# Other places in the instruction streams for four small pieces of a fused retention and MLP kernel: the first constants, a first ScalarE copy, the splits of the feature halves, the loads of the second weight

## The chip, the cores and the metric

The kernel runs on one core of one Trainium2 chip. The metric is the device time of one execution in microseconds (us); several runs are taken and their median is given. Besides them one execution is recorded by the hardware profiler, and every row below is from that execution. An engine is named as the profile names it: PE is TensorE's matmuls, PEld its weight loads, DVE is VectorE, ACT is ScalarE, POOL is GpSimd, and SP is SyncE, the engine that issues all DMAs of this kernel (SPq is its queue).

## The reference, cut to what matters

```python
# retention: 4 batches, 8 heads, 576 positions, 64 dims per head
ret = (q @ k.T / sqrt(64)) * gamma[h] ** (i - j)   # zero above the diagonal
x = ret @ v                                        # (4, 576, 512)
# first MLP with a spatial gate
h = gelu_tanh(x @ w_in); u, v = halves(h)
v = (v - mean) / sqrt(var + 1e-6) * g_ln
x = x + (u * (w_sg @ v + b_sg)) @ w_out
# second MLP
xn = (x - mean) / sqrt(var + 1e-6) * g_ln
out = x + relu(xn @ w_ch1) @ w_ch2                 # 512 -> 2048 -> 512
```

Everything is fp32. The kernel computes each product of the two MLPs as three matmuls of split operands, hi*hi + hi*lo + lo*hi, where hi is a rounded copy of an operand and lo the remainder. Such a split costs an ACT copy (hi) and a DVE or POOL subtraction (lo).

## The kernel before, in words

**Retention (about the first 90 us).** Sixteen units (4 batches by 4 pairs of heads) are worked on one after the other. A unit needs its tile of q, k and v, called ld (`load_unit`, L183), and the constants of its pair of heads, called tab (`load_tab`, L432): decay masks and scales. `prep_unit` (L195) scales k on ACT with a column of tab (L207), `scores` (L209) multiplies k and q on PE (L219) and masks the result on DVE with tab (L224), `states` (L234) builds the running state from the scaled k (PE L240, ACT L246, DVE L248), and `attend` (L263) puts the pieces together. Unit 0 is loaded in three pieces: half of the positions of q and k (256 KB), the other positions (320 KB), the rest of the tile (544 KB). Every other unit is one DMA of 1120 KB, and every tab one of 225.5 KB. At the start the order on SP is: unit 0, tab 0, unit 1, tab 1, unit 2, tab 2, tab 3 (L435 to L438). Then DVE zeroes a tile and PE multiplies it three times (L440 to L444) before the first unit is prepared.

**First MLP (to about 311 us).** It is not touched by the change.

**Second MLP (from about 311 us).** The 18 row tiles are cut into 3 blocks (`NB`), and each block takes 8 steps (`NQ`). A step s makes two chunks of 128 hidden features for 768 rows: `hidden` (L946) computes them by a 7-product scheme (Strassen's, on 2 by 2 blocks) in four parts, and `project` (L975) multiplies the hidden chunks of step s - 1 by their part of w_ch2. The loop over s has an inner loop over four quarters q (L1050 to L1075). In a quarter the program emits one part of `hidden`, one `project`, and then the preparation of weights: in quarter 0 `split_w2` and `load_w2` of one half of w_ch2 and the first part of `split_w1` (ACT L727, DVE L728), in quarter 1 the second part of `split_w1` (ACT L727, POOL L728) and `load_w1`, in quarter 2 `split_w2` and `load_w2` of the other half, in quarter 3 the four POOL sums of `mix_w1` (L714 to L718) for the weights of step s + 2. `split_w2` is an ACT copy (L741) and a POOL subtraction (L742); `load_w2` (L730) is one DMA of 256 KB into one of two buffers, the one that the split before it has read. w_ch2 is loaded three quarters or more before it is split.

Last in a quarter comes `ahead(blk, q)` (L1009), where q now counts the 32 quarters of a block. It prepares the next block: rows are loaded and normed, their transposes written to DRAM (L765) and read back (L777), scaled (L785), and in the last quarters of a block turned into the 7 operands of the scheme. Four of the operands are differences (`mix_features`, L796, POOL L799, called m0 to m3 here), and each of the 7 is split (`split_features`, L802, ACT L806 and DVE L807): first the plain quarter b11, then m0, m1, m2, m3, then the plain b21 and b22. In block 0 `ahead` also does the last of the conversions of w_ch from 64-bit to 32-bit (DVE L142 to L151, written to DRAM by L371), whose buffers are given to the operands of block 1 at its quarter 24 (L1028 to L1034).

All engines run their instructions in the order in which the program emits them, so the place of a call in this loop is its place in the queue of its engine. In part (1, 2) of `hidden`, DVE adds product 2 from a PSUM bank (L964), and the next part goes on accumulating into that same bank, so PE has to wait for that L964.

Of the kernel before, what the change touches and what calls it, by code (L numbers as in the profile page):

```python
# [21 lines left out]
NP = H // 2  # L22
# [69 lines left out]
def kernel(  # L92
# [12 lines left out]
    nc = tc.nc  # L105
    ctx.enter_context(tc.manual_schedule())
    act, dve, pool, pe = nc.scalar, nc.vector, nc.gpsimd, nc.tensor
# [51 lines left out]
    def bank():  # L159

        return banks.popleft()
# [13 lines left out]

    tab = [pa.tile([128, TA], F32, tag=f"tab{hp}", bufs=1, name=f"tab{hp}") for hp in range(NP)]

    NU = B * NP
    units = {}
    xb = {}  # L180
# [2 lines left out]
    def load_unit(n):  # L183
        t = ld.tile([128, AW], F32, tag="ld", name="ld")
        if n == 0:

            to, src = (z[:, 0:2 * S].rearrange("p (a s) -> p a s", a=2) for z in (t, attn[n]))
            for x, y in ((0, 2 * C), (2 * C, S)):
                nc.sync.dma_start(out=to[:, :, x:y], in_=src[:, :, x:y])
            nc.sync.dma_start(out=t[:, 2 * S:], in_=attn[n, :, 2 * S:])  # L190
        else:
            nc.sync.dma_start(out=t, in_=attn[n])
        units[n] = dict(ld=t)
# [235 lines left out]
            mm3(ps, hi[:, k, c], lo[:, k, c], wi[k][:, 0, 512:], wi[k][:, 1, 512:], k == 0, k == KE - 1)  # L429
        return ps  # L430

    def load_tab(hp):  # L432
        nc.sync.dma_start(out=tab[hp], in_=tab_in[hp])

    for n in range(3):  # L435
        load_unit(n)
        load_tab(n)
    load_tab(NP - 1)  # L438

    zero = pa.tile([128, 512], F32, tag="p", name="zero")  # L440
    dve.memset(zero, 0.0)
    warm = bank()
    for _ in range(WARM):
        pe.matmul(warm, zero[:, 0:128], zero, start=True, stop=True)  # L444
# [4 lines left out]
    states(0)  # L449
    for n in range(NU):  # L450
        if n + 3 < NU:
            load_unit(n + 3)
# [277 lines left out]
    def load_w2(s):  # L730
        if s < NB * NF:
            if t2 is None:
                w2_raw[s] = x_raw[2][:, WQ - 1024 + s * 512:WQ - 1024 + (s + 1) * 512]
            else:
                w2_raw[s] = t2.tile([128, 512], F32, tag="w2", bufs=2, name="raw_w2")
            nc.sync.dma_start(out=w2_raw[s], in_=w2_dram[s % NF // 2 + NQ * (s % 2)])

    def split_w2(s):
        if s < NB * NF:
            raw, t = w2_raw.pop(s), w2_at[s % 2]  # L740
            act.copy(t[:, 0], raw)  # L741
            pool.tensor_tensor(out=t[:, 1], in0=raw, in1=f(t[:, 0]), op=ALU.subtract)  # L742
# [266 lines left out]
    def ahead(blk, q):  # L1009

        tick()
        background(int(PACE[B][q % 4]) if blk == 0 and q > 3 else 0)
        n = (blk + 1) * TB
        if q == 1 and blk:
            for j in reversed(range(TB // 2, TB)):
                load_rest((blk - 1) * TB + j)
        if blk + 1 < NB:
            for j in range(TB):
                at = 3 + 5 * j // 2
                if q == at:  # L1020
                    load_y(n + j)
                if q == at + 1:
                    norm(t2, n + j)
            if q in (13, 20):
                load_features(blk + 1, q // 20)
            if q in (15, 22):
                scale_features(blk + 1, q // 20)
            if q == 24 and blk == 0:  # L1028
                for _ in bg:
                    pass  # L1030
                es_d.close()
                t = ctx.enter_context(tc.tile_pool(name="t4", bufs=1, side="right", reuse_waits="tile"))
                t = t.tile([128, 28 * TH], F32R, tag="fe", name="fe")
                fe[1] = [[t[:, (2 * i + a) * 2 * TH:(2 * i + a + 1) * 2 * TH] for a in range(2)] for i in range(7)]  # L1034
            if q == 24:
                feat[:] = mix_features(blk + 1), split_features(blk + 1)
            if q == 25:
                next(feat[0])
            if q >= 25:
                next(feat[1])  # L1040
                if q > 25:
                    next(feat[0], None)
        if q == 4 * NQ - 1:
            for j in reversed(range(TB // 2)):
                load_rest(blk * TB + j)
# [4 lines left out]
    for s in range(NB * NQ + 1):  # L1050
        steps = hidden(s) if s < NB * NQ else None
        for q in range(4):
            if steps:
                next(steps)
            if s:
                project(s - 1, q)

            if q == 0 and s > 1:
                split_w2(2 * s - 1)
                load_w2(2 * s + 1)  # L1060
            if q == 2 and s:
                split_w2(2 * s)
                load_w2(2 * s + 2)
            if q < 2 and s:
                split_w1(s + 1, q)
            if q == 1:
                load_w1(s + 2)
            elif q == 3:
                mix_w1(s + 2, 0)
                mix_w1(s + 2, 1)  # L1070
            if steps:
                ahead(*divmod(4 * s + q, 4 * NQ))
            elif q == 0:
                for j in reversed(range(TB // 2, TB)):
                    load_rest((NB - 1) * TB + j)  # L1075
# [57 lines left out]
```

## Time and profile before

| | before |
|---|---|
| median of 3 runs | 709.73 us |
| lowest, highest | 708.83, 713.69 us |
| the profiled execution, own time | 708.72 us |
| span of its profile | 706.8 us |
| PE busy | 670.8 us (95%) |
| DVE busy | 501.8 us (71%) |
| ACT busy | 288.8 us (41%) |
| POOL busy | 339.7 us (48%) |
| moved by DMA | 116.96 MB, mean 165 GB/s |
| granted TensorE clock, mean | 0.987 |

Times in rows count from the start of the span. A row of the timeline names the start, the duration, the engine, the line and operation, what is written and read, and in brackets how long the engine was idle before it and what ended that. A granted clock of 1.00 is the full 2.4 GHz, and 0.50 is 1.2 GHz. The profiled execution's own time is 1.9 us above its span.

### The profile page before, as it was taken

Reading aid. Unit: us, or ns where it says so; the run is one execution under the profiler, and the core shown is the slowest. Engines: PE = TensorE matmul, PEld = TensorE weight load, DVE = VectorE, ACT = ScalarE, POOL = GpSimd, SP = SyncE. Lnnn points to the kernel's source line nnn. Section 1 sums busy time; section 2 is a strip of 40 time slices with the busy share of each in tenths; the row PEclk is TensorE's granted clock in tenths of the full one; section 3 lists DMA queues with packets and bytes.
Section 4 is the critical chain, followed back from the end, with each engine's and each line's share of the span. In section 5 each row is a group of like instructions: output and inputs, shape, how many; then the busy total and the mean of one; then the engine's idle time right before and its main releaser. Section 6 shows DMA issues by size and latency. Waiting matters only on the chain.

```text
span 706.8 us, 11642 instructions
## 1 busy us (share of the span) xinstructions
PE 670.8 (95%) x4294; PEld 594.4 (84%) x4294; DVE 501.8 (71%) x961; ACT 288.8 (41%) x528; POOL 339.7 (48%) x302
## 2 busy tenths in 40 slices
PE   7978997999899989999999998999999899999997
PEld 4866787889789869988878887989888789898985
DVE  2999798999998988786888766667655654434333
ACT  2433355335326436443444544333544433333221
POOL 0321545613714543975555577454456754444411
PEclk9999999999999999999999999999999999999999
DMA  8887636486586659554474513634542154122132
GB/s 334 329 318 290 203 102 189 151 272 186 188 272 207 199 161 246 179 166 162 165 210 147 135 60 105 224 132 132 137 120 75 45 167 146 60 88 78 30 120 89
DMA packets 61960, 116.96 MB, mean 165 GB/s; under 512 B 6480, under 2 KB 25936, under 8 KB 59984
## 3 DMA queue, kind: packets, MB, share of 16 engines
q1 hardware_dynamic: 61904, 116.23, 51.3%
q8 instruction: 33, 0.54, 0.3%
q14 instruction: 23, 0.19, 0.1%
HBM read 88.16 MB, written 27.26 MB: 163 GB/s over the span
## 4 chain that ended last, share of the span: by engine, by line
PE 49%; DVE 30%; DMA 5%; POOL 5%; issue 5%; ACT 5%; SPq 0%; DVEq 0%; ACTq 0%; POOLq 0%
PE b L124 15%; PE b L126 15%; PE b L125 14%; DVE c L146 4%; DVE c L151 3%; DVE c L142 3%; DVE c L149 3%; PE b L674 3%; POOL mix L799 3%; DVE p L224 2%; DVE bs L489 2%; DMA rows<-y_dram 1%; DVE b L610 1%; DVE u L613 1%; DVE y L248 1%
## 5 line engine op out<-in xcount | busy, mean ns | idle before, releaser
L124 PE MATMUL b<-fe,w 128*128 128x384 f32 x336 | 115.2, 343 | 5.7 <-DVE t L964 3.7
L742 POOL TENSOR_TENSOR w<-raw_w,w 128x512 fp32r<-128x512 f32 x46 | 63.1, 1373 | 112.1 <-ACT w L741 112.1
L126 PE MATMUL b<-w,h 128*128 128x512 f32 x288 | 114.7, 398 | 0.0
L124 PE MATMUL b<-w,h 128*128 128x512 f32 x288 | 114.4, 397 | 0.0
L125 PE MATMUL b<-w,h 128*128 128x512 f32 x288 | 114.1, 396 | 0.0
L125 PE MATMUL b<-fe,w 128*128 128x384 f32 x336 | 114.0, 339 | 0.0
L126 PE MATMUL b<-fe,w 128*128 128x384 f32 x336 | 113.9, 339 | 0.0
L941 ACT ACTIVATE h<-b 128x384 fp32r<-128x384 f32 x72 | 35.3, 491 | 161.8 <-DVE b L969 120.2
L124 PEld LDWEIGHTS b<-fe,w 128*128 128x128 f32 x336 | 63.3, 188 | 13.6 <-DVE t L964 5.0
L942 DVE SCALAR_TENSOR_TENSOR h<-b,h 128x384 fp32r<-128x384 f32 x72 | 40.0, 556 | 47.6 <-ACT h L941 47.6
L728 POOL TENSOR_TENSOR w<-raw_w,w 128x768 fp32r<-128x768 f32 x23 | 43.4, 1888 | 53.7 <-ACT w L727 50.5
L125 PEld LDWEIGHTS b<-fe,w 128*128 128x128 f32 x336 | 63.6, 189 | 3.6
L126 PEld LDWEIGHTS b<-w,h 128*128 128x128 f32 x288 | 54.5, 189 | 13.2
L126 PEld LDWEIGHTS b<-fe,w 128*128 128x128 f32 x336 | 63.5, 189 | 0.0
L148 ACT ACTIVATE raw<-raw 128x512 f32<-128x512 f32 x44 | 30.0, 681 | 81.2 <-DVE c L146 67.0
L125 PEld LDWEIGHTS b<-w,h 128*128 128x128 f32 x288 | 54.6, 190 | 9.5
L124 PEld LDWEIGHTS b<-w,h 128*128 128x128 f32 x288 | 54.6, 190 | 8.9
L969 DVE TENSOR_TENSOR b<-b,u 128x384 f32<-128x384 f32 x48 | 26.9, 561 | 40.1 <-PE b L126 39.8
L494 POOL TENSOR_TENSOR st<-st,par 128x1 f32<-128x1 f32 x36 | 24.7, 687 | 52.1 <-DVE st L493 45.6
L727 ACT CAST w<-raw_w 128x1024 fp32r<-128x1024 f32 (+1 forms) x47 | 44.2, 943 | 12.7 <-POOL raw_w L718 7.9
L384 POOL TENSOR_TENSOR xt_lo<-xb,xt_hi 128x576 fp32r<-128x576 f32 x16 | 24.6, 1545 | 47.4 <-ACT xt_hi L383 47.4
L728 DVE TENSOR_TENSOR w<-raw_w,w 128x1024 fp32r<-128x1024 f32 x24 | 35.2, 1466 | 13.2 <-ACT w L727 13.1
(135 smaller groups left out, 1612.8 us busy)
## 6 DMA issues: line engine op xcount, KB each, us to landing
ld<-in_attn_dram SPq DMA_DIRECT2D x15, 1120.0 KB, 7.1
raw<-in_w_ch_dram SPq DMA_DIRECT2D x32, 512.0 KB, 4.5
raw_w<-w_dram SPq DMA_DIRECT2D x24, 512.0 KB, 3.9
raw_w<-w_dram SPq DMA_DIRECT2D x46, 256.0 KB, 2.6
w_dram<-c SPq DMA_DIRECT2D x32, 256.0 KB, 2.5
row<-y_dram SPq DMA_DIRECT2D x30, 256.0 KB, 4.2
x_r<-x_dram SPq DMA_DIRECT2D x18, 256.0 KB, 4.4
y_dram<-x_r SPq DMA_DIRECT2D x18, 256.0 KB, 3.0
```

The costliest lines, as they stand in the source:

```text
L124: pe.matmul(ps, lh, rh, start=first, stop=False, skip_group_check=True)
L125: pe.matmul(ps, lh, rl, start=False, stop=False, skip_group_check=True)
L126: pe.matmul(ps, ll, rh, start=False, stop=last, skip_group_check=True)
L146: dve.scalar_tensor_tensor(out=c, in0=w1, scalar=0xC0000000, in1=c, op0=ALU.bitwise_and, op1=ALU.bitwise_or)
L148: act.activation(out=f(w1), in_=f(w1), func=ACTF.Square)
L494: pool.tensor_tensor(out=st[:, 3:4], in0=st[:, 2:3], in1=col(par, O_MH), op=ALU.pow)
L727: act.copy(hi, r)
L728: (pool if s and part else dve).tensor_tensor(out=lo, in0=r, in1=f(hi), op=ALU.subtract)
L742: pool.tensor_tensor(out=t[:, 1], in0=raw, in1=f(t[:, 0]), op=ALU.subtract)
L941: act.activation(out=t[:, 0], in_=v, func=ACTF.Relu)
L942: dve.scalar_tensor_tensor(out=t[:, 1], in0=v, scalar=0.0, in1=f(t[:, 0]), op0=ALU.max, op1=ALU.subtract)
L969: dve.tensor_tensor(out=v, in0=v, in1=u, op=ALU.add)
```

## The change

Four edits, with no arithmetic changed:

1. tab 0 is issued right behind the first piece of unit 0's q and k, and every other tab ahead of the unit that uses it.
2. ACT copies one column of the zeroed tile onto itself before the three matmuls on zeros.
3. `split_features` begins a quarter earlier, at q = 24, leaves out q = 28 and ends where it did. `mix_features` begins at q = 24 too.
4. `load_w2` is called a quarter after `split_w2`, not right behind it.

```diff
+    def load_tab(hp):
+        nc.sync.dma_start(out=tab[hp], in_=tab_in[hp])
...
             for x, y in ((0, 2 * C), (2 * C, S)):
                 nc.sync.dma_start(out=to[:, :, x:y], in_=src[:, :, x:y])
+                if x == 0:
+                    load_tab(0)
             nc.sync.dma_start(out=t[:, 2 * S:], in_=attn[n, :, 2 * S:])
...
-    def load_tab(hp):
-        nc.sync.dma_start(out=tab[hp], in_=tab_in[hp])
-
     for n in range(3):
         load_unit(n)
-        load_tab(n)
-    load_tab(NP - 1)
+        load_tab(n + 1)

     zero = pa.tile([128, 512], F32, tag="p", name="zero")
     dve.memset(zero, 0.0)
+
+    act.copy(zero[:, 0:1], zero[:, 0:1])
     warm = bank()
...
             if q == 24:
                 feat[:] = mix_features(blk + 1), split_features(blk + 1)
-            if q == 25:
+
+            if q == 24:
                 next(feat[0])
-            if q >= 25:
+            if q >= 24 and q != 28:
                 next(feat[1])
-                if q > 25:
+                if q > 24:
                     next(feat[0], None)
...
             if q == 0 and s > 1:
                 split_w2(2 * s - 1)
+            if q == 1 and s > 1:
                 load_w2(2 * s + 1)
             if q == 2 and s:
                 split_w2(2 * s)
+            if q == 3 and s:
                 load_w2(2 * s + 2)
```

The first place is SP at the start of the program; ld is the tile of a unit (128x2x256 and 128x2x320 are the two pieces of q and k, 128x1088 the rest), tab_95 to tab_98 are the constants of pairs 0 to 3. Before:

```order
L189 DMA ld<-in_attn_dram 128x2x256
L189 DMA ld<-in_attn_dram 128x2x320
L190 DMA ld<-in_attn_dram 128x1088
L433 DMA tab_95<-in_tab_dram 128x451
L192 DMA ld<-in_attn_dram 128x2240
L433 DMA tab_96<-in_tab_dram 128x451
L192 DMA ld<-in_attn_dram 128x2240
L433 DMA tab_97<-in_tab_dram 128x451
```

And in the changed kernel:

```order
L192 DMA ld<-in_attn_dram 128x2x256
L179 DMA tab_95<-in_tab_dram 128x451
L192 DMA ld<-in_attn_dram 128x2x320
L195 DMA ld<-in_attn_dram 128x1088
L179 DMA tab_96<-in_tab_dram 128x451
L197 DMA ld<-in_attn_dram 128x2240
L179 DMA tab_97<-in_tab_dram 128x451
L197 DMA ld<-in_attn_dram 128x2240
```

tab 0 moved from the fourth place to the second, and each later tab passed the 1120 KB tile of a unit.

The second place is DVE in steps 6 and 7 of block 0 (quarters 24 to 29); fe is the lo part of an operand of the next block, w the lo part of w_ch1, h, t and u are pieces of `hidden`. Before:

```order
L962 TENSOR_TENSOR u<-b_75,u 128x384
L728 TENSOR_TENSOR w_3473<-raw_w_4221,w_3472 128x1024
L942 SCALAR_TENSOR_TENSOR h<-b_75,h 128x384
L964 TENSOR_TENSOR t<-b_76,u 128x384
L807 TENSOR_TENSOR fe<-x,fe 128x768
...
L962 TENSOR_TENSOR u<-b_75,u 128x384
L728 TENSOR_TENSOR w_3378<-raw_w_4350,w_3377 128x1024
L807 TENSOR_TENSOR fe<-mix,fe 128x768
L942 SCALAR_TENSOR_TENSOR h<-b_75,h 128x384
L964 TENSOR_TENSOR t<-b_76,u 128x384
L807 TENSOR_TENSOR fe<-mix,fe 128x768
```

And in the changed kernel, where L965, L731, L945, L967 and L810 are the lines L962, L728, L942, L964 and L807 of before:

```order
L965 TENSOR_TENSOR u<-b_75,u 128x384
L731 TENSOR_TENSOR w_3474<-raw_w_4222,w_3473 128x1024
L810 TENSOR_TENSOR fe<-x,fe 128x768
L945 SCALAR_TENSOR_TENSOR h<-b_75,h 128x384
L967 TENSOR_TENSOR t<-b_76,u 128x384
...
L965 TENSOR_TENSOR u<-b_75,u 128x384
L731 TENSOR_TENSOR w_3379<-raw_w_4354,w_3378 128x1024
L945 SCALAR_TENSOR_TENSOR h<-b_75,h 128x384
L967 TENSOR_TENSOR t<-b_76,u 128x384
L810 TENSOR_TENSOR fe<-mix,fe 128x768
```

In step 7 (second piece) no split stands between the weights' lo part and L967 any more; in step 6 (first piece) one now does.

## Rows read from the trace of the kernel before

**Rows 1.** The page: busy time and share of each engine.

```profile
PE 670.8 (95%) x4294; PEld 594.4 (84%) x4294; DVE 501.8 (71%) x961; ACT 288.8 (41%) x528; POOL 339.7 (48%) x302
```

**Rows 2.** Busy time by stretch: window, length, each engine's busy time (instructions), clock, DMA.

```profile
434.00:546.00 112.00, 111.92 (x554) 99.99 (x554) 70.07 (x128) 47.19 (x81) 59.85 (x58) 1.00 0.45 137
564.00:694.00 130.00, 129.92 (x641) 116.00 (x640) 55.98 (x89) 42.26 (x74) 56.31 (x52) 1.00 0.28 94
```

**Rows 3.** Waits of PE in 311 to 706 us: total, times, longest.

```profile
PE b L124 <- DVE t L964: 3.7, 2, 1.9
```

**Rows 4.** Timeline of PE in steps 6 and 7 of block 0.

```profile
401.10 0.34 PE L124 MATMUL b<-fe,w 128*128 128x384 f32 x1
...
409.59 0.34 PE L124 MATMUL b<-fe,w 128*128 128x384 f32 x1
...
416.97 0.34 PE L124 MATMUL b<-fe,w 128*128 128x384 f32 x1
...
427.45 0.45 PE L124 MATMUL b<-fe,w 128*128 128x384 f32 x1 [1.86 <-DVE t L964]
```

**Rows 5.** Busy time by stretch, behind three waits of PE.

```profile
428.00:433.00 5.00, 5.00 (x19) 4.47 (x18) 3.21 (x4) 1.50 (x3) 1.92 (x2) 0.66 0.20 82
558.00:563.00 5.00, 5.00 (x19) 4.54 (x18) 3.20 (x4) 1.46 (x3) 1.97 (x2) 0.66 0.21 88
369.00:375.00 6.00, 5.15 (x27) 4.54 (x26) 4.67 (x10) 5.18 (x10) 3.40 (x4) 1.00 0.80 256
```

**Rows 6.** Timeline of DVE in steps 6 and 7 of block 0.

```profile
404.83 1.68 DVE L728 TENSOR_TENSOR w<-raw_w,w 128x1024 fp32r<-128x1024 f32 x1
...
408.69 2.04 DVE L807 TENSOR_TENSOR fe<-x,fe 128x768 fp32r<-128x768 f32 x1 [0.44 <-ACT fe L806]
...
414.84 1.42 DVE L807 TENSOR_TENSOR fe<-mix,fe 128x768 fp32r<-128x768 f32 x1 [0.69 <-ACT fe L806]
...
422.70 1.78 DVE L728 TENSOR_TENSOR w<-raw_w,w 128x1024 fp32r<-128x1024 f32 x1 [1.94 <-ACT w L727]
424.40 2.06 DVE L807 TENSOR_TENSOR fe<-mix,fe 128x768 fp32r<-128x768 f32 x1
426.38 0.55 DVE L942 SCALAR_TENSOR_TENSOR h<-b,h 128x384 fp32r<-128x384 f32 x1
426.85 0.54 DVE L964 TENSOR_TENSOR t<-b,u 128x384 f32<-128x384 f32 x1
```

**Rows 7.** Timeline of ACT in steps 6 and 7 of block 0.

```profile
407.82 0.84 ACT L806 CAST fe<-x 128x768 fp32r<-128x768 f32 x1
...
421.62 1.05 ACT L727 CAST w<-raw_w 128x1024 fp32r<-128x1024 f32 x1 [1.88 <-POOL raw_w L718]
```

**Rows 8.** SP's last write of converted w_ch: timeline.

```profile
404.29 0.32 SPq L371 DMA_DIRECT2D w_dram<-c  x1
```

**Rows 9.** The same write among the DMA issues: KB, us to landing.

```profile
w_dram<-c SPq DMA_DIRECT2D x1, 256.0 KB, 2.1
```

**Rows 10.** The chain of waits, 0 to 14 us: start, us, what.

```profile
2.24 6.83 DMA tab<-in_tab_dram
```

**Rows 11.** DMA issues, 2.7 to 3.1 us (unit 1).

```profile
ld<-in_attn_dram SPq DMA_DIRECT2D x1, 1120.0 KB, 9.1
```

**Rows 12.** Timeline of ACT, 0 to 13 us.

```profile
9.14 1.28 ACT L207 ACT_TABLE_LOAD   x1 [9.14 <-DMA tab<-in_tab_dram]
10.44 0.91 ACT L207 ACTIVATE ld<-ld,tab 128x256 f32<-128x256 f32 x2
12.44 0.91 ACT L207 ACTIVATE ld<-ld,tab 128x256 f32<-128x256 f32 x2 [1.09 <-DMA tab<-in_tab_dram]
```

**Rows 13.** Timeline of PE, 10 to 14 us.

```profile
12.01 1.68 PE L219 MATMUL b<-ld 64*128 64x128 f32 x16
```

**Rows 14.** Waits of SP's queue: total, times, longest.

```profile
SPq L765 <- DVE st L493: 28.4, 7, 8.8
```

**Rows 15.** The page: DMA issues, KB each, median us to landing.

```profile
raw_w<-w_dram SPq DMA_DIRECT2D x46, 256.0 KB, 2.6
```

## The prediction

> **What bounds the kernel now.** I read the busy times first: PE works 95% of the span [rows 1], so an edit is worth something only where PE stands still or runs slowly. The busy times by stretch come next: from 434 to 546 us and from 564 to 694 us PE is busy without a gap to speak of, at the full clock [rows 2], so what is won or lost at 425 us or 557 us arrives whole at the end. Then PE's waits in the second MLP: two waits on DVE L964, 3.7 us together [rows 3]. The timeline puts the first at 427.45 us, after 1.86 us of idleness [rows 4]; the second stands 130 us later, in block 1, and takes the other 1.8 us. They are the same place of the program, step 7 of a block, quarter 29. Behind each the clock falls: it is 0.66 in the mean from 428 to 433 and from 558 to 563 us with PE busy throughout, that is 1.2 GHz for some 3.4 us of each stretch, and 5.0 x 0.34 = 1.7 us of work are lost each time [rows 5]. A boundary between blocks costs 1.8 + 1.7 = 3.5 us, and both together 7.1 us.
>
> Why L964 is late stands in DVE's timeline [rows 6]. The weights' lo part (L728) starts at 422.70 us, since ACT L727 waited for POOL until 421.62 us [rows 7]. Behind it DVE runs the split of m2 (L807, 2.06 us), and only then L942 and L964, which ends at 427.39 us.
>
> **The split a quarter earlier, step 7.** Quarter 28 has no split any more. POOL's work ahead of ACT L727 stays as long as it was: m2 stands before the four sums of quarter 27 where m1 stood. So L728 starts near 422.7 us still; L942 and L964 follow it directly, and L964 ends near 427.39 - 2.0 = 425.4 us. PE reaches the place at 427.45 - 1.86 = 425.59 us. The wait is gone with 0.2 us to spare, and with it the cause of the slow stretch. I book 3.5 us in each of the two blocks that have a successor: 7.1 us.
>
> **What it adds: step 6.** The split of b11 now stands between L728 and L964 in quarter 24, where there was none. PE needs that L964 at 409.59 us [rows 4], 8.5 us after the step's beginning at 401.10. In block 0 the split has a wait that was covered until now: the operand's memory is that of the last converted piece of w_ch, which must have been written out. SP issues that write at 404.29 us [rows 8] and it lands 2.1 us later [rows 9], at 406.4. ACT L806 then takes 0.84 us [rows 7], to 407.3, where before it ran at 407.82 behind other work and the wait was not seen. Queued behind it on ACT is the relu of quarter 25, which L942 needs; on DVE, L942 and L964 themselves stand behind the split. The split takes 1.42 us alone and 2.04 us beside POOL's subtractions [rows 6], so it ends at 408.8 to 409.4 us; L942 and L964 take 0.47 + 0.54 = 1.0 us, and L964 ends at 409.8 to 410.4. PE waits 0.2 to 0.9 us. POOL has m0 and L728 there, so I take 0.7, near the upper end. A wait of 0.85 us (5.15 busy of 6 us from 369 us) left the clock at 1.00 [rows 5], so I book no slow stretch. As bounds: no wait at all if DVE runs it alone and early, and 3.2 us plus a slow stretch of 1.7 if the write lands late (rival below).
>
> In block 1 there is no such write. ACT can copy b11 right behind L727, and DVE runs the split behind L728, which took 1.68 us from 404.83 in the twin step [rows 6]: 404.83 + 1.68 + 2.04 + 1.0 = 409.55 us against the 409.59 at which PE comes. I book 0, with 0.5 us as the upper bound.
>
> The other splits keep their quarters, as m0 is split where b11 was, and so on; m3, b21 and b22 don't move. POOL has m0 at quarter 24, in a gap that it had, and its load at quarter 28 is less. In block 0 all of step 7 shifts with PE by 0.7 us; whether L728 shifts by more is worth 0 to 0.6 us, of which I take 0.1.
>
> **The start.** The table load (1.28 us) ran on ACT after tab 0 had landed at 9.07 us [rows 10, 12]. Ahead of the warm-up it waits for nothing and is over before 2 us. The copy makes the warm-up wait some 0.5 us, which shifts the first scores and no more, since PE then has nothing to do until the scaled k is there. tab 0 comes earlier, but ACT L207 also needs the rest of unit 0. Before, 256 + 320 + 544 + 225.5 = 1345.5 KB had been asked for by tab 0's end, landed at 9.07; in the new order the rest of unit 0 closes the same 1345.5 KB, so I put it at 9.1 us. L207 starts then and not at 10.44: 1.3 us earlier, and PE's states likewise.
>
> What is late next is unit 1. It was issued at 2.71 us and landed 9.1 us later [rows 11], at 11.8, as byte 2465.5 KB; tab 1 behind it landed at 12.4, where ACT's second pair of L207 starts [rows 12], as byte 2691 KB. In the new order tab 1 goes first and unit 1 is the one that ends 2691 KB, so it lands at 12.4. ACT's second L207 starts where it did. PE's scores of unit 1, at 12.01 before [rows 13], start 0.4 us later. The gain of 1.3 us is given back whole. I book a loss of 0.2 us, since part of the 0.4 goes into PE work that waited for ACT anyway; the bounds are a loss of 0.6 and a gain of 1.4 us.
>
> One rule bears on the size of what could be won here. The row shows that an ACTIVATE follows the table load at once: 9.14 + 1.28 = 10.42, and it starts at 10.44 [rows 12]. The Trainium skill, page "ScalarE: Activation LUTs", section "What ACT_TABLE_LOAD costs", counts a switch of the table as about 1.28 us of loading and 1.38 us of draining, 2.66 in all. By the page the gain open to the rival below would be 1.4 us larger; the row shows no drain at this first load, and the sum goes by the row.
>
> **The loads of w_ch2.** 46 DMAs of 256 KB move behind whatever the quarter issues on SP between: rows, transposes, converted weights, outputs. Three quarters remain from the load to its split. A step is 416.97 - 401.10 = 15.9 us [rows 4], so that is 11.9 us, and a load lands after 2.6 us [rows 15]. What stood behind a blocked load on SP goes out earlier, yet the waits of PE that the view lists for this part are on DVE, none on a DMA. I book 0, with 0.5 us either way.
>
> **The sum.** The profiled execution took 708.7 us. 708.7 - 7.1 + 0.7 + 0.1 + 0.2 = 702.6. Its own time is 1.0 us under the median of the runs, 709.73, and 0.1 under their lowest; I add half a microsecond and forecast 703.1 us, 0.9% faster than the median. A measurement of this kernel can tell about 1% from no change, so this falls just inside.
>
> **Rivals.**
>
> *The start pays too.* If the transfers share the engines so that tab 1 slips through beside unit 1, the 1.3 to 1.4 us stay: 703.1 - 1.6 = 701.5 us, or 700.9 if the wait in step 6 is hidden as well. For it: tab 1 landed only 0.6 us after unit 1 although it is a separate transfer asked for later, so they overlap. Against it: tab 0 to tab 3 and the units landed in the order in which they were issued.
>
> *Block 0 pays for the earlier split.* If the write of w_ch takes not 2.1 us but twice that, L806 ends at 409.3, L964 at 412.4 or so, and PE waits 2.8 us and then runs slowly: 4.5 us instead of 0.7, which makes 706.9. It decides from a wait of over some 1.5 us. For it: unit 1, issued among other transfers, took 9.1 us to land [rows 11], so landings stretch where the engines are shared. Against it: at 404 us the queue has just been idle for some microseconds.
>
> *Nothing comes of it.* If the same wait only moves from quarter 29 to quarter 25, in both blocks, with the clock falling as before, the time stays at 709.7. For it: DVE has the same work in the same two steps. Against it: in step 6 L728 begins 3.7 us after the step's beginning, and in step 7 it is 5.7 [rows 4, 6], so DVE has 2.0 us more there.
>
> *The loads come too late: slower.* On SP everything waits for what is in front. The longest wait of the queue for the write of a transposed row is 8.8 us [rows 14]. A load that stands behind such a wait lands after 8.8 + 2.6 = 11.4 us of the 11.9 that it has; from half a microsecond more on, ACT L741 holds up the relus behind it, and PE waits. With 1.9 us of waiting and 1.7 us of slow clock as at the boundaries, five steps of block 0 or 1 make 18 us: 703.1 + 18 = 721 us. Against it: the seven waits add up to 28.4 us, so the usual one is 4, and the load it would hit is mostly issued in another quarter.
>
> **Chances.** The forecast 0.57 (its own range is 702.0 to 704.8), the start pays 0.18, block 0 pays 0.13, nothing comes of it 0.07, slower 0.05. Under the 1% line (702.6 us) lie most of the first rival and a corner of the forecast: 0.25. Slower by over 1% is the last rival alone: 0.05. Within 1%: 0.70. For 8 in 10 the range takes in the first two rivals: 700.6 to 707.6 us.
>
> **What would show it.** Right: no wait of PE on L967 near 425 and 555 us, the clock at 1.00 in both stretches of 5 us, a wait of PE of under 1 us near 410 us, released by L967, ACT's second pair of scalings at about 12.4 us. Wrong: a clock under 0.9 near 411 us, or a wait of PE of over 1 us in step 7; unit 1's scores before 11.5 us; a wait of PE that goes back to ACT's copy of w_ch2 and from there to a DMA.

## The result and the profile after

The changed kernel takes 704.01 us in the median of 4 runs (701.67 to 704.57), the kernel before in the same comparison 710.84 us (4 runs). The ratio is 0.9895, 95% interval 0.9851 to 0.9938: 1.05% faster. The forecast was 703.1 us. The profiled execution took 704.57 us with a span of 702.6 us, 4.2 us under that of before.

Lines moved by a few numbers: L945, L965 and L967 of the new kernel are L942, L962 and L964 of before, L810 and L809 the split L807 and L806, L731 and L730 the weights' split L728 and L727, L717 the sum L714, L739 and L711 the loads L736 and L708, L802 the difference L799, L492 the statistics L489, L212, L224, L229 and L245 are L207, L219, L224 and L240, L376 is L371.

PE's waits in the second MLP, which answer to [rows 3] (us in total, times, longest):

```profile
PE b L124 <- DVE h L945: 1.2, 3, 0.9
PE b L124 <- DVE t L967: 0.7, 1, 0.7
PE b L124 <- DVE u L965: 0.6, 1, 0.6
```

Both waits of step 7 are gone, and one new one is there on L967 (the kernel before has the other two lines too, with 1.0 and 0.6 us). The windows over the boundaries between blocks and over the long stretches, which answer to [rows 2, 5] (busy time and instructions of each engine, then granted clock, DMA share, GB/s), and two more windows for what follows:

```profile
12.00:16.00 4.00, 4.00 (x78) 3.57 (x77) 2.17 (x6) 1.68 (x6) 0.00 (x0) 1.00 1.01 418
220.00:240.00 20.00, 16.90 (x104) 16.10 (x103) 17.10 (x48) 12.45 (x24) 8.42 (x9) 0.83 0.59 165
409.00:416.00 7.00, 6.30 (x33) 5.36 (x31) 6.42 (x8) 2.80 (x5) 7.00 (x3) 1.00 0.37 114
428.00:433.00 5.00, 5.00 (x26) 4.17 (x25) 3.49 (x6) 1.04 (x3) 3.61 (x2) 1.00 0.45 157
434.00:546.00 112.00, 112.00 (x556) 100.20 (x555) 72.35 (x130) 47.79 (x82) 62.95 (x59) 1.00 0.45 137
558.00:563.00 5.00, 5.00 (x25) 4.28 (x24) 3.11 (x5) 2.29 (x5) 3.12 (x3) 1.00 0.28 83
564.00:694.00 130.00, 130.00 (x640) 115.98 (x639) 53.29 (x86) 40.39 (x71) 53.64 (x50) 1.00 0.28 89
```

Where 0.66 stood, 428 to 433 and 558 to 563 us now show 1.00, and the long stretches behind them are as full as before, so what was won arrives at the end. The new wait is where it was forecast, in step 6 of block 0, and costs what was forecast; PE's row there:

```profile
412.87 0.44 PE L124 MATMUL b<-fe,w 128*128 128x384 f32 x1 [0.70 <-DVE t L967]
```

To see where time goes between two traces, the same instructions of both were set side by side and their starts subtracted: I call this the lag of the new kernel, negative when it is ahead. It is worked out from many rows, by the medians of PE's and ACT's instructions near a time:

| place (time in the kernel before) | lag of the new kernel, us |
|---|---|
| 70 us, in the retention | +0.11 |
| 160 us | +0.18 |
| 220 to 390 us, first MLP and after | +1.89 to +2.14 |
| 417 us, behind the new wait | +3.36 |
| 445 us, behind the first boundary | -0.39 |
| 541 us | -0.35 |
| 575 us to the end | -4.15 |

Each boundary gives 3.8 us, step 6 takes 1.2 (0.9 of it at the new wait), the start gives nothing, and 1.7 us are lost between 160 and 220 us in the first MLP, which no edit touches. Of these 1.4 us stand in one place, where DVE waits for a load; in the kernel before the same instruction (L489 at 219.09 us) has no wait:

```profile
220.97 0.69 DVE L492 BATCH_NORM_STATS2 bs<-rows 128x6 f32<-128x512 f32 x1 [1.34 <-DMA rows<-y_dram]
```

The clock of 0.83 from 220 to 240 us (1.00 in the kernel before) cost nothing that lasted: DVE's lag is +1.89 at 220 us and +1.88 at 240.

### The profile page after: what moved, and what is told of

Read it like the earlier page. It is cut to its first block, busy times and chain, and to the rows that moved or that the text cites. A ratio compares the mean times of both kernels' runs of the same rounds, so it can differ in the third digit from the quotient of the medians.

```text
span 702.6 us, 11640 instructions
## 1 busy us (share of the span) xinstructions
PE 671.4 (96%) x4294; PEld 595.3 (85%) x4294; DVE 500.2 (71%) x961; ACT 289.5 (41%) x529; POOL 343.1 (49%) x302
## 4 chain that ended last, share of the span: by engine, by line
PE 53%; DVE 30%; DMA 6%; issue 5%; ACT 4%; SPq 1%; POOL 0%; DVEq 0%; ACTq 0%
PE b L124 16%; PE b L126 16%; PE b L125 16%; DVE c L146 4%; PE b L677 4%; DVE c L151 4%; DVE c L149 3%; DVE c L142 3%; DMA ld<-in_attn_dram 2%; DVE p L229 2%; DVE bs L492 1%; DMA raw<-in_w_ch_dram 1%; DVE b L613 1%; DVE y L253 1%; DVE u L616 1%
## 5 line engine op out<-in xcount | busy, mean ns | idle before, releaser
L944 ACT ACTIVATE h<-b 128x384 fp32r<-128x384 f32 x72 | 35.4, 491 | 160.2 <-DVE b L972 121.7
L945 DVE SCALAR_TENSOR_TENSOR h<-b,h 128x384 fp32r<-128x384 f32 x72 | 40.1, 556 | 45.6 <-ACT h L944 45.5
L731 POOL TENSOR_TENSOR w<-raw_w,w 128x768 fp32r<-128x768 f32 x23 | 45.9, 1996 | 47.8 <-ACT w L730 44.5
L730 ACT CAST w<-raw_w 128x1024 fp32r<-128x1024 f32 (+1 forms) x47 | 44.2, 943 | 13.2 <-POOL raw_w L721 8.5
L731 DVE TENSOR_TENSOR w<-raw_w,w 128x1024 fp32r<-128x1024 f32 x24 | 34.7, 1447 | 14.5 <-ACT w L730 14.5
```

Source lines behind the costliest of these rows:

```text
L730: act.copy(hi, r)
L731: (pool if s and part else dve).tensor_tensor(out=lo, in0=r, in1=f(hi), op=ALU.subtract)
L944: act.activation(out=t[:, 0], in_=v, func=ACTF.Relu)
L945: dve.scalar_tensor_tensor(out=t[:, 1], in0=v, scalar=0.0, in1=f(t[:, 0]), op0=ALU.max, op1=ALU.subtract)
```

## The experiments

Ratios are to the kernel before on the same chip, with the 95% interval. The lags are again against the profiled execution of before, and that one is slow at the start: at 80 us DVE is 0.7 to 1.6 us ahead of it in the five other executions with the old start (e1, e3, e5, e9, e13). A lag of about that size in the retention says nothing on an edit; the step that a lag makes over a boundary is not touched by it.

### e1: the splits alone

The diff is the third piece of the change (the `split_features` and `mix_features` lines), on the kernel before; so its line numbers are those of before.

> Only the earlier splits (edit 3), on the kernel before. Theory (the boundaries between blocks make the whole gain): both waits of about 1.85 us on DVE L964 in step 7 and the slow clock behind them are gone, 7.1 us; a wait of 0.2 to 0.9 us comes in step 6 of block 0; the time is 6 to 7 us below the kernel before, ratio about 0.991. Rival (the start or the loads made a good part of it): 3 to 5 us, ratio 0.993 to 0.996, and the rest shows in the run with the other edits.

Measured: 700.97 us against 710.18, ratio 0.9881 (0.9856 to 0.9906). The boundaries give 3.8 us each in the lag (-0.16 to -3.97, -3.95 to -7.79), as in the whole change. So edit 3 alone is all of the gain that the times can show. One thing differs from the whole change: the new wait of step 6.

```profile
409.26 0.44 PE L124 MATMUL b<-fe,w 128*128 128x384 f32 x1 [0.20 <-DVE t L964]
```

0.20 us and not 0.70. The rest of the experiments say why.

### e2: the start alone

Edits 1 and 2 on the kernel before (here L944 and L966 are L942 and L964, L809 and L808 the split L807 and L806, L971 is L969).

> Only the order of the first DMAs and the first ACT copy (edits 1 and 2), on the kernel before. Theory: what the first scaled k gains is given back before 60 us, since unit 3 lands later and DVE is busy without a gap from 24 us on; the time is within 1 us of before, and DVE is within 0.3 us of before at 60 us. Rival (the start pays): 1.4 us or more stay at 60 us, and the time is 1.4 us lower.

Measured: 709.41 us, ratio 0.9989 (0.9974 to 1.0003). The lag is -0.52 at 30 us and -0.05 at 100 us: the start gives nothing that can be told from no change. Its profile shows something I had not looked for. The boundary's first wait is there as in [rows 4], but the clock does not fall:

```profile
424.00:428.00 4.00, 3.90 (x20) 3.14 (x18) 3.00 (x2) 2.92 (x4) 4.00 (x3) 1.00 0.00 0
428.00:433.00 5.00, 3.26 (x17) 3.08 (x18) 3.36 (x5) 0.83 (x1) 4.25 (x2) 1.00 0.43 157
433.00:437.00 4.00, 3.01 (x15) 2.34 (x14) 2.16 (x6) 2.26 (x4) 0.72 (x1) 1.00 0.01 4
```

In its place PE waits a second and a third time:

```profile
429.74 0.44 PE L124 MATMUL b<-fe,w 128*128 128x384 f32 x1 [1.83 <-DVE t L966]
435.18 0.45 PE L124 MATMUL b<-fe,w 128*128 128x384 f32 x1 [0.99 <-DVE t L966]
440.10 0.44 PE L124 MATMUL b<-fe,w 128*128 128x384 f32 x1 [0.43 <-DVE h L944]
```

These are 3.25 us in all (in block 1 1.86, 0.95 and 0.45), and the lag does not change over the boundary (+2.36 at 395 us, +2.34 at 445): with or without the slow clock the boundary costs the same. The reason stands on DVE:

```profile
429.14 0.54 DVE L966 TENSOR_TENSOR t<-b,u 128x384 f32<-128x384 f32 x1
431.32 1.75 DVE L809 TENSOR_TENSOR fe<-mix,fe 128x768 fp32r<-128x768 f32 x1 [1.64 <-ACT fe L808]
432.99 0.55 DVE L971 TENSOR_TENSOR b<-b,u 128x384 f32<-128x384 f32 x1
434.11 0.56 DVE L944 SCALAR_TENSOR_TENSOR h<-b,h 128x384 fp32r<-128x384 f32 x1 [0.56 <-ACT h L943]
434.58 0.55 DVE L966 TENSOR_TENSOR t<-b,t 128x384 f32<-128x384 f32 x1
```

From one L966 to the next DVE takes 434.58 - 429.14 = 5.44 us: it waits 1.64 us for ACT's copy of m3 and then splits it. In the kernel before it is 432.24 - 426.85 = 5.39 us, with the same 1.64 us in it:

```profile
429.03 1.71 DVE L807 TENSOR_TENSOR fe<-mix,fe 128x768 fp32r<-128x768 f32 x1 [1.64 <-ACT fe L806]
430.66 0.55 DVE L969 TENSOR_TENSOR b<-b,u 128x384 f32<-128x384 f32 x1
...
432.24 0.55 DVE L964 TENSOR_TENSOR t<-b,t 128x384 f32<-128x384 f32 x1
```

So in the kernel before PE at half speed just filled the time that it would have waited at full speed. In the changed kernel the same stretch takes 431.87 - 428.31 = 3.56 us, for m3 was mixed in quarter 27, ACT's copy of it is ready by 427.95 us, and its split follows at once:

```profile
428.31 0.54 DVE L967 TENSOR_TENSOR t<-b,u 128x384 f32<-128x384 f32 x1
428.77 1.13 DVE L810 TENSOR_TENSOR fe<-mix,fe 128x768 fp32r<-128x768 f32 x1
...
431.87 0.55 DVE L967 TENSOR_TENSOR t<-b,t 128x384 f32<-128x384 f32 x1
```

5.39 - 3.56 = 1.83 us. That is the second half of the boundary's gain, and it comes from the operand of quarter 29 being ready, not from the clock. Here it is ready since `mix_features` is a quarter earlier on POOL; e8 gets it another way.

### e3 and e4: the loads alone, and the start with the loads

e3 is edit 4 alone on the kernel before (its lines are those of before), e4 edits 1, 2 and 4 without the splits.

> Only the later loads of w_ch2 (edit 4), on the kernel before. Theory: no effect, within 0.7 us of before, both waits on L964 stay at about 1.85 us. Rival (the later loads hold up the load of w_ch1 behind them on SP, and with it POOL's sums): POOL L714 in step 6 of block 0 waits for its DMA by 0.5 us or more longer than before, the wait in step 7 grows by as much, and the time is 0.5 to 1.5 us higher.

> The change without the earlier splits (edits 1, 2 and 4). Theory: within 1 us of before. Rival (the parts help each other): 2 us or more below before.

Measured: e3 709.4 us, ratio 0.9988 (0.9973 to 1.0003); e4 709.86 us, ratio 0.9997 (0.9982 to 1.0012). In both the two waits of step 7 stay (in e3 3.7 us, 2 times, 1.9 the longest), with a clock of 0.66 to 0.69 behind them. What the rival of e3 looked for is there in part: POOL's first sum of step 6 (L714) waits 0.66 us for its load in e3 and 1.01 in e4, against 0.15 in the kernel before; but the waits of step 7 did not grow by it, nor did the time. Neither edit is worth anything that can be told from no change while the boundary is as it was.

### e5: half a split a quarter later

All seven splits where they were, but the split of m2 (operand 6 in the code's count) cut: one half in quarter 28, the other in quarter 29 in front of m3's. L964 then stands behind half a split, while step 7 has as much DVE work as before (here L970 is L964 and L948 is L942).

```diff
-            dve.tensor_tensor(out=lo, in0=y, in1=f(hi), op=ALU.subtract)
-            yield
+            if i == 6 and blk:
+                dve.tensor_tensor(out=lo[:, 0:1], in0=y[:, 0:1], in1=f(hi)[:, 0:1], op=ALU.subtract)
+                yield
+                dve.tensor_tensor(out=lo[:, 1:2], in0=y[:, 1:2], in1=f(hi)[:, 1:2], op=ALU.subtract)
+            else:
+                dve.tensor_tensor(out=lo, in0=y, in1=f(hi), op=ALU.subtract)
+            if i != 6 or not blk:
+                yield
```

> The kernel before, but in quarter 28 DVE splits only half of m2 and does the other half in quarter 29 (the subtraction L807 in two instructions of 128x384 instead of one of 128x768). L942 and L964 of step 7 then have about 1 us less in front. Theory 1 (the slow clock is a price of its own on top of the wait): the wait is 0.8 to 0.9 us, the clock stays at 1.00 over the five us behind it, and each boundary gets 1.0 + 1.7 = 2.7 us cheaper, 5.4 us in all. Theory 2 (DVE is behind by a fixed amount there, and what the wait or the slow clock does not use up comes as another wait behind it, as in the run with edits 1 and 2 alone, where the clock stayed up and waits of 0.95 to 0.99 us and 0.4 us followed): each boundary gets 1 us cheaper or less, since the other half still stands in DVE's queue one quarter on, and waits of PE appear behind the first; 2 us in all.

Measured: 709.0 us against 708.93, ratio 0.9999 (0.9978 to 1.0019). The clock is 1.00 in 428 to 433 and 558 to 563 us, and PE waits three times, 1.44 + 1.28 + 0.42 = 3.14 us:

```profile
428.45 0.44 PE L124 MATMUL b<-fe,w 128*128 128x384 f32 x1 [1.44 <-DVE t L970]
434.19 0.45 PE L124 MATMUL b<-fe,w 128*128 128x384 f32 x1 [1.28 <-DVE t L970]
439.09 0.44 PE L124 MATMUL b<-fe,w 128*128 128x384 f32 x1 [0.42 <-DVE h L948]
```

Half the split saved 0.39 us at the first place (against e2's 1.83: it takes 1.66 us, where the whole took 2.05), and the other half gave 0.29 of it back at the second. Why half the work saved so little stands on POOL. Here are the half split and POOL's instruction beside it, then that POOL instruction in the kernel before, where the whole split stands at 424.40 us [rows 6]:

```profile
424.75 2.29 POOL L742 TENSOR_TENSOR w<-raw_w,w 128x512 fp32r<-128x512 f32 x1
425.81 1.66 DVE L808 TENSOR_TENSOR fe<-mix,fe 128x384 fp32r<-128x384 f32 x1
```

```profile
423.36 2.29 POOL L742 TENSOR_TENSOR w<-raw_w,w 128x512 fp32r<-128x512 f32 x1
```

POOL's instruction ends at 427.04 us and the half split at 427.47, 0.42 behind it; in the kernel before they end at 425.65 and 426.46, 0.81 apart. So it is everywhere: all 292 whole splits of the 14 traces start while a POOL instruction is running, and each ends 0.81 to 0.87 us behind the end of that instruction; the four halves of e5 end 0.41 or 0.42 behind it. Only the part behind POOL goes with the size, and that part shrank by 0.39 us. PE follows: it starts 1.80 us behind the end of POOL's L742 in the kernel before (425.65, 427.45), 1.81 in e2.

In e5 what step 7 costs, DVE's surplus of work and waiting in it, stayed when a part of a split moved within the step. It went where work left the step (e1, e8, e9).

### e9: the earlier splits in block 1 only

```diff
-            if q == 25:
+            first = 24 if blk else 25
+            if q == first:
                 next(feat[0])
-            if q >= 25:
+            if q >= first and not (blk and q == 28):
                 next(feat[1])
-                if q > 25:
+                if q > first:
                     next(feat[0], None)
```

> The kernel before, with the earlier splits in block 1 alone; block 0 keeps its old quarters. Theory: the first boundary keeps its wait of about 1.85 us and what follows it, the second loses it; half of the gain of the splits, 3.5 to 4.2 us below before. Rival (the boundaries depend on each other): the gain is under 2 us or the second boundary keeps a wait of over 0.5 us.

Measured: 704.78 us against 708.93, ratio 0.9938 (0.9916 to 0.996), half of e1's gain. Its profile has one wait on L964 left (1.86 us at 426.41), and the two boundaries read:

```profile
428.00:433.00 5.00, 5.00 (x20) 4.43 (x19) 3.76 (x5) 1.69 (x4) 0.98 (x2) 0.70 0.00 2
558.00:563.00 5.00, 5.00 (x27) 4.30 (x25) 3.00 (x4) 2.96 (x5) 3.70 (x4) 1.00 0.32 86
```

The two boundaries are independent, and each is worth 3.8 us (the lag stays at -1.03 over the first and goes from -1.01 to -4.85 over the second).

### e7 and e8: ACT's order at the start, and a later last split

I thought then that ACT's order gives the start's gain back: it scales k of unit n + 2 (waiting for its tile) ahead of the small copies that unit n + 1 needs. e7 has edits 1, 2 and 3, without 4, and turns this round. e8 has the same start, the splits in quarters 25, 26, 27, 29, 30 and 31, and the last (b22) in quarter 1 of the next block; its `mix_features` stands in quarters 25 to 28, as before.

```diff
     scores(0)
-    prep_unit(1)
     states(0)
+    prep_unit(1)
...
-        if n + 2 < NU:
-            prep_unit(n + 2)
         if n + 1 < NU:
             scores(n + 1)
...
             states(n + 1)
+        if n + 2 < NU:
+            prep_unit(n + 2)
         attend(n)
```

> Edits 1, 2 and 3 (the loads of w_ch2 as before), and in the retention ACT scales the k of the next unit but one behind the copy that DVE's running state waits for, and not ahead of it. Theory (the gain of the start is given back because unit 3's tile lands at 19.6 us and ACT's copy L251 is queued behind the scaling that waits for it): DVE's waits for ACT's copy in the first 60 us, 5.6 us in the changed kernel, fall under 1 us, DVE is 1.5 to 2.5 us ahead of the kernel before at 60 us, and the time is 1.5 to 2.5 us below the run with the splits alone. Rival (the DMAs bound the retention): DVE waits for PE in place of ACT, and it is within 0.5 us of before at 60 us.

> As the run with the scaling behind the copy, but the splits stay off both quarters that begin a step: b11 at quarter 25, m0 at 26, m1 at 27, m2 at 29, m3 at 30, b21 at 31, and b22, which is needed last, in quarter 1 of the next block. Theory: PE has no wait on L964 at all, neither in step 6 nor in step 7 (0.2 us in the run with the splits alone), and none of over 0.3 us in the first step of the next block; 0.2 to 0.7 us below the run with the scaling alone, which the times cannot tell. Rival (the two splits in a row at quarter 31 and the next quarter 1 make a new wait): a wait of 0.5 us or more on DVE in the first step of block 1.

Measured: e7 702.24 us, ratio 0.9905 (0.9877 to 0.9933); e8 701.64 us, ratio 0.9898 (0.9871 to 0.9925). Neither can be told from e1. In e7 DVE's waits for ACT in the first 60 us fell as expected, from 5.6 us in the changed kernel to 0.5, but DVE is only 0.6 us ahead of before at 60 us and 0.1 behind at 100: now it waits 2.1 us for the load of w_in (L142), and 9.4 for PE's scores where it was 7.1. So ACT's order alone was not what took the gain. Yet e8, with the same start, is 2.5 us ahead at 60 us and 2.0 at 100.

In e8 the wait of step 6 is gone, and the boundaries give 3.7 us each (+0.70 to -3.02 and -2.99 to -6.69), although m3 is mixed in quarter 28 as in the kernel before. Quarter 29 splits m2 here, which is ready, and it waits for nothing (L809 is L807):

```profile
426.02 1.12 DVE L809 TENSOR_TENSOR fe<-mix,fe 128x768 fp32r<-128x768 f32 x1
```

Another wait of 1.69 us stands at 377.85 us, behind a DVE conversion (L149) that took 2.33 us where e1 has 0.68. It starts 0.07 us behind a POOL instruction that runs to 376.32 us; in e1 it starts 0.55 us ahead of that instruction. In this execution the place costs 2.3 us (lag -1.53 at 340 us, +0.76 at 390), more than the later split gained.

### e10 to e13: the third unit's tile, and the loads, on one chip

e11 has edits 1, 2 and 3 (no 4), e12 is the changed kernel again, e13 the splits alone again. e10 is e11 with the first load of w_in one unit later:

```diff
-        if n == 0:
+        if n == 1:
             background(1)
```

> Edits 1, 2 and 3 without 4, and the first load of w_in (512 KB, issued at 6.9 us in the changed kernel) asked for one unit later, behind unit 4's tile. Theory (the start is bound by the delivery of unit 3's tile, which shares the DMA engines with that load): unit 3's tile lands about 512 KB / 415 GB/s = 1.2 us earlier, at 18.4 us in place of 19.64, ACT's scaling of unit 3 follows it, and at 30 us the kernel is 1 to 1.4 us ahead of e11; the time is 1 to 1.5 us under e11. Rival 1 (ACT's order, not the tile, gives the start back): the tile lands earlier and ACT's scaling of unit 3 does not, or nothing is left at 30 us; the same time as e11. Rival 2 (w_in is late next): DVE L142 waits for the raw weights at about 24 us, 1 us or more, and the gain is lost by 60 us.

> Edits 1, 2 and 3 without edit 4. Theory (edit 4 delays load_w1 and with it the earlier split in block 0): the wait of PE in step 6 of block 0 falls from 0.70 us to about 0.2, as in e1, so 0.5 us under e12 (the changed kernel), ratio near 0.988 to 0.989. Rival (the start edits cause the 0.7 by shifting the conversions of w_ch): the wait stays at 0.6 to 0.8 us and the time equals e12's.

> The changed kernel itself, to stand beside e10, e11 and e13 on one chip. Both theories: ratio to before 0.988 to 0.991, about 0.5 us over e11 by the theory of the loads, equal to it by its rival.

> Edit 3 alone again, beside the whole change on one chip. Theory (the split is the whole gain, the start and the loads give nothing): within 0.2% of e12, at or a little under it. Rival (the start's 1.8 us survive in most executions and the profiled one was an exception): e12 is faster than e13 by 1 to 2 us.

| | median of 6, us | ratio (before: 709.16) | wait of PE in step 6, us | ACT scales unit 3 at, us | lag at 45 us |
|---|---|---|---|---|---|
| e10 | 704.13 | 0.9929 (0.9902 to 0.9956) | 0.19 | 18.65 | +1.87 |
| e11 | 702.81 | 0.9906 (0.9878 to 0.9933) | 0.22 | 18.58 | -2.16 |
| e12 (the change) | 702.88 | 0.9910 (0.9885 to 0.9935) | 0.79 | 19.83 | -0.23 |
| e13 (old start) | 702.74 | 0.9916 (0.9888 to 0.9944) | 0.27 | 18.41 | -0.75 |

The loads: the wait is 0.70 and 0.79 us in the two executions with edits 3 and 4, and 0.19 to 0.27 in four with edit 3 and not 4 (e1, e10, e11, e13; e7 has none). The first sum on POOL for the step shows the cause, in the changed kernel:

```profile
403.17 0.74 POOL L717 TENSOR_TENSOR raw_w<-raw_w 128x256 f32<-128x256 f32 x1 [0.99 <-DMA raw_w<-w_dram]
```

It waited 0.99 us for `load_w1`, in e12 0.72, in e11 0.15 (with edit 4 and no splits 0.66 in e3 and 1.01 in e4). On SP the 256 KB load of w_ch2 (L739) now goes out right in front of those 512 KB (L711), where it stood 4 us ahead of them before (390.67 and 394.78 us):

```profile
396.93 0.41 SPq L739 DMA_DIRECT2D raw_w<-w_dram  x1
397.39 0.43 SPq L711 DMA_DIRECT2D raw_w<-w_dram  x1
```

So edit 4 costs about half a microsecond in step 6, by trace; in the medians (e11 and e12: 0.1 us apart) half a microsecond does not show. The delay reaches PE by way of POOL's m0 (L802), which stands behind the sums. These are the rows of the changed kernel, then those of e1 (L799, L806, L807 and L964 there):

```profile
408.14 1.23 DVE L731 TENSOR_TENSOR w<-raw_w,w 128x1024 fp32r<-128x1024 f32 x1 [1.25 <-ACT w L730]
408.21 2.85 POOL L802 TENSOR_TENSOR mix<-x 128x768 f32<-128x768 f32 x1
409.39 2.50 DVE L810 TENSOR_TENSOR fe<-x,fe 128x768 fp32r<-128x768 f32 x1
412.27 0.54 DVE L967 TENSOR_TENSOR t<-b,u 128x384 f32<-128x384 f32 x1
```

```profile
404.63 2.83 POOL L799 TENSOR_TENSOR mix<-x 128x768 f32<-128x768 f32 x1
405.62 0.84 ACT L806 CAST fe<-x 128x768 fp32r<-128x768 f32 x1 [1.58 <-DMA w_dram<-c]
406.50 1.78 DVE L807 TENSOR_TENSOR fe<-x,fe 128x768 fp32r<-128x768 f32 x1 [0.74 <-ACT fe L806]
408.67 0.54 DVE L964 TENSOR_TENSOR t<-b,u 128x384 f32<-128x384 f32 x1
```

PE comes to its place at 412.17 us in the changed kernel and at 409.06 in e1 (the start of its matmul less its wait). The split of b11 starts no later: 2.78 us ahead of that in the changed kernel, 2.56 in e1. But m0 starts half a microsecond later, 3.96 us ahead of it and 4.43, and the split ends 0.83 and 0.82 us behind m0's end (411.06 and 407.46). So the split takes 2.50 us in place of 1.78. PE starts 1.80 or 1.81 us behind the end of m0 in all six executions that have this wait (the change, e1, e10, e11, e12, e13).

The start: e10 was a miss. Its tile of unit 3 was there by 18.65 us, but so was e11's at the old place of the load (6.08 + 12.42 = 18.50 us), and the moved load was missed later:

```profile
31.08 0.43 DVE L142 TENSOR_SCALAR c<-raw 128x512 uint32<-128x512 uint32 x1 [0.88 <-DMA raw<-in_w_in_dram]
```

What e11 shows beside e12 (and e8 beside e7) is that one and the same start can be 2 us ahead of before (lag -2.16) or not (-0.23); in e11 and e12 it goes with unit 3's tile. The old start does as much by itself: e3 is 1.6 us ahead at 80 us.

## Why the prediction was right, point by point

**What bounds the kernel, and the boundary's price.** Right: PE's full stretches handed the gain on to the end, and e1 and e13 show that edit 3 makes it. The price was 3.5 us a boundary; it measured 3.8 in the lag (a place where PE waits loses 0.2 to 0.3 us more than the wait in brackets: the wait of 0.70 us moved PE's lag from +2.42 to +3.36). But one step of the reasoning was wrong: "The wait is gone with 0.2 us to spare, and with it the cause of the slow stretch". The 1.7 us that I read as work lost to 1.2 GHz [rows 5] were also what DVE was late by at the next L964. e2 and e5 have the wait without the slow clock and lose as much. Had edit 3 only moved the split within step 7, the sum would have been wrong by most of its 3.5 us a boundary, to judge by e5, where half a split moved and 0.1 us was won (lag +1.42 to +1.34). It came out because the same edit also mixes m3 a quarter earlier, which I had noted only as less load on POOL. So the size of that half, 1.7 us a boundary, was luck.

**Step 6.** The wait of 0.7 us came as 0.70, under a clock of 1.00, but not by the working given. The write went as worked out: it landed after 2.0 us, as in [rows 9], and in e1 ACT's copy starts at 405.62 us, which is within 0.1 us the 406.4 of the forecast less e1's lead of 0.7. But it is not the write and the copy that set the end of the split; that is the end of POOL's m0. The 1.42 us that I read as the split "alone" [rows 6] is no such thing, for POOL's L742 runs there from 414.15 to 415.44 us, and the split takes 2.50 us in the changed kernel, over the upper end of my 2.04. POOL's m0 was my reason for the 0.7, and that much was right. With edit 3 alone the wait is 0.2 us (e1), the lower end of my 0.2 to 0.9; the other half microsecond is edit 4's, which I had booked at 0. The rival in which block 0 pays did not come. In block 1 no PE wait appears, as booked.

**The loads of w_ch2.** Booked at 0, with 0.5 us either way; by the traces 0.5 us lost, the edge of that. I looked for a load that would come late itself, and the harm is to the load behind it, by way of POOL. The slower rival did not come: no wait of PE goes back to the copy of w_ch2.

**The start.** Right in size (the forecast loses 0.2, the lag says +0.1 at 70 us), as far as one execution of each can tell. The rows of the changed kernel look better than forecast: ACT's first scaling of k starts at 8.46 us, 2.0 us earlier and not 1.3, and unit 1, which I had land at 12.4 us, was there at 11.7:

```profile
8.46 0.91 ACT L212 ACTIVATE ld<-ld,tab 128x256 f32<-128x256 f32 x2 [6.25 <-DMA ld<-in_attn_dram]
11.74 0.91 ACT L212 ACTIVATE ld<-ld,tab 128x256 f32<-128x256 f32 x2 [2.37 <-DMA ld<-in_attn_dram]
15.07 0.91 ACT L212 ACTIVATE ld<-ld,tab 128x256 f32<-128x256 f32 x2 [2.33 <-DMA ld<-in_attn_dram]
19.70 0.91 ACT L212 ACTIVATE ld<-ld,tab 128x256 f32<-128x256 f32 x2 [3.62 <-DMA ld<-in_attn_dram]
```

The second and third scalings are 0.7 us earlier than before (12.44 and 15.77), the fourth is 0.6 us later (19.09), since unit 3's tile landed at 6.13 + 13.49 = 19.62 us. But a good part of this is the execution that I compared with. I worked by bytes: what closes the first 1345.5 KB lands at 9.1 us, what closes 2691 KB at 12.4, in either order. With the old order the six traces have the first at 8.40 to 9.07 us and the second at 11.68 to 12.36, and the kernel before has the latest of both; with the new order the eight traces have 7.90 to 8.60 and 11.19 to 11.97. So the new order is some 0.4 us earlier in the mean of each, and the step is wrong by that much and not by 0.7. In the mean the first scaling is 1.6 us earlier (8.07 to 8.69 us in the six traces with the new start and ACT's old order, 9.77 to 10.44 with the old start) and the second 0.3 us (11.41 to 12.06 against 11.76 to 12.44): most of it is given back there, as forecast. What comes behind is not explained: the DMA engines are full there (their share is 1.01 at 418 GB/s from 12 to 16 us, and 1.04 at 425 in the kernel before). My sign of being wrong (unit 1's scores before 11.5 us) was near: they start at 11.70.

**The sum.** Terms and measurement in the profiled executions: boundaries -7.1 forecast, -7.6 measured; step 6 +0.8, +1.2; start and loads +0.2, +0.1 by 70 us. That makes -6.1 and -6.3 us. The profiled execution gained only 4.2, because the first MLP, which nothing touches, ran 1.7 us longer up to 220 us (1.4 of it the load that DVE waits for), and 0.2 more by 390. That is scatter of this stretch: between 160 and 220 us the lag changes by +0.5 in e12, the same kernel, by -1.3 in e9 and by +1.2 in e5. The medians do not carry it: 710.84 - 704.01 = 6.8 us.

**The chances.** I gave 0.70 to "within 1%" and 0.25 to faster by more. The ratio of 0.9895 lies just on the far side, and its interval (0.6% to 1.5%) holds the line, as do those of e1 (0.9881) and e12 (0.991).

**What stays open.** Unit 3's scaling starts between 18.0 us (e2) and 19.8 (e12) in kernels whose start is the same; what sets that was not found. The three with edit 4 have it late (19.70 in the change, 19.71 in e4, 19.83 in e12) and the three without it, with the same order on ACT, early (18.01 in e2, 18.58 in e11, 18.65 in e10), but edit 4 moves nothing before 311 us, and e7 and e8, without it, have 19.43 and 19.14; so no cause is shown. An early tile is not enough either: e2 and e10 had it, and at 60 us e2 was 0.3 us ahead and e10 1.9 behind. Nor does the clock of PE from 12 to 16 us sort them: the changed kernel has 1.00 and is not ahead, e3 has 0.63 and is. Whether the start gains a microsecond in the mean can't be told from 6 runs a kernel; with 12 runs e2 says 0.1% faster, and its interval goes from 0.3% faster to no change. Nor is a version shown that beats the change: e1 (0.9881), e7, e8, e11 and e13 all lie within its interval. The plainest, e1, needs one of the four edits.

## What to carry to other kernels

Where an engine ran late over a whole step, the first wait that it caused was not the price. So take the late engine's timeline over the next two or three points where it is waited for, and ask how much work leaves the step, for a slow clock behind a wait can be time that would have been waited anyway. Read the time of a DVE instruction together with the POOL instruction that it falls on: here the end of POOL's set the end of DVE's. A load that is moved is judged by the load which it is now in front of, not only by its own due time. One trace of before is one draw: where the same stretch is in five other traces, look at its scatter there before explaining a microsecond of it.

## What the runs showed of the hardware that was not expected

The same wait of PE, 1.83 to 1.86 us behind the same instruction with the same matmuls ahead of it, stands at nine boundaries. It was followed by 1.2 GHz for part of the next 5 us at seven (both of the kernel before, of e3 and of e4, and the first of e9: 0.66 to 0.70 in the mean) and by the full 2.4 GHz at both of e2 (1.00). The time of the boundary was the same, as DVE was late in each.

DVE's subtraction of 128x768 in the splits took 0.95 to 2.61 us, always started beside a running POOL instruction, and ended 0.81 to 0.87 us behind the end of that one, in 292 of 292 cases; half of it (128x384) took 1.66 and 1.23 us and ended 0.41 or 0.42 behind. How long such a subtraction took was set by what was left of the POOL instruction that it fell on, more than by its own size.

A DMA of 1120 KB in the first microseconds, asked for at 5.7 to 6.1 us behind the same nine others, took 12.42 us to land in e11 and 14.06 in e12.
